# Split output weights for all twelve channel blocks in the last batch, eight factor sets, and a planner that knows more of what a product waits for

## The chip, the cores and the metric

One core of a Trainium2 chip runs the whole kernel. The metric is the device time of one execution in microseconds (us). The profile below is of one execution; the other times are of runs without it. Lower is better.

## The reference

An attention block with 32 inducing points feeds a SwiGLU block. There are 4 batches of 12416 rows with 128 channels, so 49664 rows go through the second block.

```python
def mab(q, kv):
    s = scale * (q @ kv.transpose(0, 2, 1))
    s = s - s.max(-1, keepdims=True)
    a = np.exp(s)
    a /= a.sum(-1, keepdims=True) + 1e-09
    return a @ kv
h = mab(I, x)            # I: 32 inducing points, x: the rows of a batch
x = mab(x, h)
...
xn = x / rms * rms_g
g = xn @ w_gate          # 128 -> 1536
silu = g * (1.0 / (1.0 + np.exp(-g)))
val = xn @ w_val         # 128 -> 1536
return (silu * val @ w_out).astype(np.float32)   # 1536 -> 128
```

## The kernel before, in words

**Work and its tiles.** A batch is cut into 7 stages of rows and these into 25 units: 24 of 512 columns (480 in the sixth stage) and one of 256. A unit passes through the second block in 12 channel blocks of 128, so a batch has 300 *slots*, one for each unit and block. In a slot (`slot`, L678) TensorE makes the gate product (L681) and the value product (L692), ScalarE the silu (L689), and VectorE multiplies the two (L698). The result, u, is one operand of the output product with the block's part of `wo`, which is summed over the 12 blocks in the PSUM tile `acc`. When a unit's twelve are in, `finish` (L622) adds and turns it, and four DMAs store it.

**Plain and split blocks.** A plain block does the output product in fp32 (`project`, L617; TensorE runs it as two instructions, so the profile counts it twice). A split block replaces it by three products of fp32r operands: `three` (L655) makes three factors (hi, lo, d) of u, and `project3` (L633) multiplies them with three parts of the weights; two go to the PSUM tile `u3`, the third to `acc`. ScalarE copies u3 when a unit's last split product is in (L642). Two kinds: by *sums*, u stays in PSUM, ScalarE makes hi (L663), VectorE lo (L664), GpSimd d (L673); by *differences*, ScalarE makes d and hi (L667, L672) and GpSimd lo and d (L668, L673). The factors lie in a ring of four sets (`RING`), in the room of x's row tiles xn2 to xn4. The weights' parts are made in slots 17 to 24 of the first batch (`split_wo`, L570) for the first ten of twelve channel blocks (`NK = NJ - 2`); blocks 10 and 11 are always plain.

**The head.** The weights come as 64-bit floats, and each of nine chunks of 512 columns is rounded to fp32 in steps (`rounding`, L214: power, power_number, upper, upper_number, sign, lower), the last of which is a multiplication on GpSimd (L283). The gate and value chunks are then multiplied with the first batch's h (`stack_of`, L469) to make the stationary operands sg and sv, and are copied to DRAM on SP's queue (`put`, L219) for the later batches. The first chunk of each lies in a borrowed tile. For the others `power` allocates "home", a tile of four chunks in the room of xn1. `stack_of` removes chunks from `w0`, and "home" is allocated again whenever the chunk (0, 1) is not in it.

**What sets the order.** Each engine executes its instructions in the order in which the program issues them, and the order is written out. `schedule` (L825) gives each step of the attention of the next batch a slot; `seam` (L487) is the rest of the attention that belongs to a stage, down to a moving operand for the gate and value products. `rehearse` (L931) goes through all slots with costs and keeps a clock for each engine. It decides which blocks are split and in which way (`decide`, L1040, with `fits`, L1026, which asks how far VectorE, ScalarE and GpSimd would fall behind), and at which place TensorE gets each output product: ahead of a slot's gate product or of its value product (`picks`). Before the value product it takes products only as long as a reserve of 7 stays over (`RESERVE`, with exceptions). Products are then issued in this order (`products`, L1144), and a product that is not ready stops all later work on TensorE.

Of the kernel before, what the change touches and what calls it, by code (L numbers as in the profile page):

```python
# [18 lines left out]
P = 128  # L19
# [4 lines left out]
def kernel(  # L24
# [189 lines left out]
    def rounding(i, c):  # L214
# [20 lines left out]
        def power():  # L235
            if i < 2:
                if not c:
                    t = silp.tile([P, 512], F32, name="silu") if i else halves.tile([P, 512], F32, name="lo")
                    w0[i, c] = t[:]
                else:  # L240
                    if (0, 1) not in w0:
                        w0["home"] = xnp.tile([P, 4, 512], F32, name="xn1")
                    w0[i, c] = w0["home"][:, 2 * (c - 1) + i, :]
                dst = st["dst"] = w0[i, c]
            else:
                dst = st["dst"] = wo.rearrange("p j c -> p (j c)")[:, ts(c, 512)]
            if not wide:
                nc.sync.dma_start(out=dst if i < 2 else dst.rearrange("p (j c) -> p j c", c=C), in_=source(i, c))
                return
            words = raw[i, c].rearrange("p (f w) -> p f w", w=2)  # L250
            st["low"], st["high"] = words[:, :, 0], words[:, :, 1]
            e = st["e"] = work.tile([P, 512], I32, name="we", tag="work")
            nc.vector.tensor_scalar(out=e[:], in0=st["high"], scalar1=20, scalar2=0x7FF,
                                    op0=ALU.logical_shift_right, op1=ALU.bitwise_and)
# [315 lines left out]
    def split_wo(step):  # L570

        if not step:
            kws["first"] = xnp.tile([P, half + NK, C], F32R, name=f"xn{full - 1}")
            for name in ("hi", "lo", "d"):
                kws[name] = xnp.tile([P, RING, 512], F32R, name=f"xn{full - 4 + len(kws) - 2}")

        def part(kind, g):
            n = kind * NK + g * half
            t = kws["first"][:, n:n + half, :] if n < half + NK else kws["more"][:, n - half - NK:n - NK, :]
            return t, t.bitcast(F32)  # L580

        def scaled(kind, g, mul, src=None):
            to, now = part(kind, g)
            nc.scalar.activation(to, now if src is None else src, AF.Copy, scale=mul)

        for g in range(2):
            one = wo[:, g * half:(g + 1) * half, :]
            at = step - g
            if at == 0:
                scaled(0, g, 1.0 - 2.0 ** -13, one)  # L590
            if at == 1:
                nc.gpsimd.tensor_tensor(out=part(1, g)[0], in0=one, in1=part(0, g)[1], op=ALU.subtract)
            if at == 3:
                scaled(1, g, 4096.0)
            if at == 4:
                nc.gpsimd.tensor_tensor(out=part(2, g)[0], in0=part(1, g)[1], in1=part(0, g)[1], op=ALU.subtract)
            if at == 6:
                scaled(0, g, 4096.0)

    def weight_of(kind, j):  # L600
        n = kind * NK + j
        return kws["first"][:, n, :] if n < half + NK else kws["more"][:, n - half - NK, :]

    def ffn(b, u):
# [28 lines left out]
        def project3(j, hi, lo, d):  # L633
            if st["k"] == nk:
                st["u"] = ps_u.tile([P, 512], F32, name="u3")
            ups = st["u"]
            nc.tensor.matmul(ups[:, 0:T], weight_of(0, j), hi, start=st["k"] == nk, stop=False)  # L637
            st["k"] -= 1
            nc.tensor.matmul(ups[:, 0:T], weight_of(1, j), lo, start=False, stop=not st["k"])  # L639
            if not st["k"]:  # L640
                o = st["o"] = outp.tile([P, 512], F32, name="o")
                nc.scalar.activation(o[:, 0:T], ups[:, 0:T], AF.Copy, scale=1.0 + 2.0 ** -12)  # L642
            project(weight_of(2, j), d)
            kws["out"] -= 1
# [10 lines left out]
        def three(j, t):  # L655

            assert kws.get("out", 0) < RING
            kws["out"] = kws.get("out", 0) + 1
            n = kws["n"] = (kws.get("n", 0) + 1) % RING
            hi, lo, d = (kws[name][:, n, 0:T] for name in ("hi", "lo", "d"))  # L660
# [9 lines left out]
            def rest():  # L670
# [3 lines left out]
                kara.append(lambda: project3(j, hi, lo, d))  # L674
# [128 lines left out]
    if B > 1:  # L803
        for _ in range(R):
# [8 lines left out]
            "lower": (0, .6, 0, 1.26), "stack_of": (.87, 0, .5), "stack_low": (0, .62), "split_wo": (0, 0, .7, 1.52)}  # L813
    BANKS = {"scores1", "sum_h", "max2", "max3", "fold_l", "turn_h", "square_h", "stack", "scores2", "square", "stack_of"}
    ENGINES = ("PE", "DVE", "ACT", "POOL")
# [9 lines left out]
    def schedule(b):  # L825
# [19 lines left out]
        if not b:  # L845
# [14 lines left out]
            marks.append(exponentials(3 * NS + 9, f["exp2"], 1))  # L860
        if b + 1 < B:
# [69 lines left out]
    def rehearse():  # L931
# [3 lines left out]
        taken = [0.0] * SILU  # L935
        queues, uses, later, left = {"plain": [], "three": []}, [0], [], {}
        split = {"out": 0, "u3": 0.0, "all": 0, "made": 0}
# [11 lines left out]
        def has(kind, by):  # L949
            return bool(queues[kind]) and queues[kind][0][0] <= by  # L950
# [4 lines left out]
        def issue(kind, to):  # L955
# [6 lines left out]
            else:  # L962
                if st["three"] == 0:
                    run("PE", 0, split["u3"])
# [4 lines left out]
                st["open"] -= 1  # L969
            st["left"] -= 1  # L970
# [3 lines left out]

        def close(unit, w):
            st = left[unit]
            if st["three"]:
                split["u3"] = run("ACT", 0.47 * w, st["end"])

            def finish():  # L980
                run("DVE", 0.6 * w, st["end"], split["u3"])
                soon(1, lambda: run("DVE", 0.63 * w))

            soon(1, finish)
# [22 lines left out]
        def do(name):  # L1007
            cost = COST.get(name, ())
            t = 0.0
            if name == "turn_z" or name == "stack_low":  # L1010
# [4 lines left out]
                return  # L1015
            i = bank() if name in BANKS else None
            for e, us in zip(ENGINES, cost):
                if us:
                    t = run(e, us, t, free[i]) if e == "PE" and i is not None else run(e, us, t)
# [20 lines left out]
        def decide(b, k, u, j):  # L1040
            n = b * NU * NJ + k
            if (j >= NK or b == 0 and (u < 2 or k < 26) or (b, u) == flat[-1] and j > 6 or split["out"] > RING or
# [6 lines left out]
        def slot(b, k, u, j, tanh):  # L1049
            w = per2[units[u][0]] * m / 512.0  # L1050
            st = left.setdefault((b, u), dict(left=NJ, three=0, open=0, all=False, slots=0, end=0.0))
            kind = decide(b, k, u, j)
            first, second = picks[b, k] = [], []
# [7 lines left out]
            least = 1 if near(b, k, 0, 4) or (b, u) == flat[-1] else RESERVE + 2 * near(b, k, -2, 0)  # L1061
# [5 lines left out]
            while split["made"] == RING and any(one[0] == 1 and one[1].__name__ == "three" for one in later):  # L1067
# [13 lines left out]
            names = [step.__name__ for step, _ in given(b, k, u, j)]  # L1081
            for name in names:
                if name in ("exp1_of", "exp2") and k in plans[b][1]:
                    run("ACT", 1.28)
                do(name)
# [27 lines left out]
            if st["slots"] == NJ:  # L1113
                st["all"] = True
                if not st["left"]:
# [9 lines left out]
    for b in range(B):  # L1125
# [3 lines left out]
        for k, (u, j) in slots(b):  # L1129

            def steps():
# [7 lines left out]
                for step, args in given(b, k, u, j):  # L1139
# [4 lines left out]
            def products(some):  # L1144
                for kind in picks[b, k][some]:
# [39 lines left out]
```

## Time and profile before

| what | value |
|---|---|
| timed runs | 1637.60, 1638.86, 1640.44 us (median 1638.86) |
| profiled execution | 1637.58 us, span of the instructions 1635.7 us |
| TensorE clock granted | 1.00 |
| silu x gate slots | 1200, of them 706 split |
| DMA traffic | 112.52 MB, 49 GB/s of HBM over the span |

Engines in the profile: PE is TensorE's matmuls and PEld its weight loads, which overlap them; DVE is VectorE, ACT ScalarE, POOL GpSimd, SP the queue that issues most DMAs. A group of instructions reads line, engine, operation, written tile <- read tiles, shapes, count | busy time, mean ns of one | idle time ahead of it and what ended it. Matmuls are pipelined, and their recorded durations overlap; the time from one start to the next shows what one costs. In the program's names, `xn` is any tile in the room of x's rows: the factors and the split weights lie there too, as does the rounded weights' "home".

### The profile page before, as it was taken

What the parts mean: (1) busy time and instruction counts of PE and PEld (TensorE: products, weight loads), DVE (VectorE), ACT (ScalarE), POOL (GpSimd) and SP (SyncE); (2) the same over time, 40 slices, a digit from 0 to 9 for tenths busy, and PEclk for the clock granted to TensorE, in tenths of its full rate; (3) what the DMA queues carried; (4) which work ended last, traced back from release to release, by engine and by line L of the source; (5) the groups of instructions that cost most, each with busy time, mean ns of one, the idle gap of its engine ahead of it and who ended that gap; (6) DMA issues with size and microseconds to landing.
All of it is one profiled execution on the core that took longest, in us unless ns stands there. A gap on an engine that the chain in (4) does not pass through costs nothing.

```text
span 1635.7 us, 25441 instructions
## 1 busy us (share of the span) xinstructions
PE 1608.4 (98%) x7086; PEld 1084.5 (66%) x7086; DVE 1444.4 (88%) x2506; ACT 1246.0 (76%) x2285; POOL 1217.5 (74%) x979
## 2 busy tenths in 40 slices
PE   8899999999999999999999999999999999999998
PEld 6546666766676666765667666676567776677776
DVE  4878988899899997889899998789989999999997
ACT  4567888767787778777778787777778788778786
POOL 1348895878588886688767897577858878878876
PEclk9999999999999999999999999999999999999999
DMA  6455534433454241624335324253221122112211
GB/s 260 90 72 81 90 62 85 102 90 63 65 88 69 40 88 26 135 58 103 63 67 84 57 39 87 49 131 77 51 38 29 29 40 38 34 35 38 39 36 27
DMA packets 389181, 112.52 MB, mean 69 GB/s; under 512 B 365072, under 2 KB 369712, under 8 KB 386480
## 3 DMA queue, kind: packets, MB, share of 16 engines
q1 hardware_dynamic: 388304, 110.82, 34.6%
q8 instruction: 56, 0.92, 0.2%
q14 instruction: 85, 0.70, 0.2%
q10 hardware_dynamic: 736, 0.08, 0.0%
HBM read 53.95 MB, written 27.00 MB: 49 GB/s over the span
## 4 chain that ended last, share of the span: by engine, by line
PE 85%; DVE 4%; issue 3%; ACT 2%; POOL 2%; DMA 1%; SPq 0%; DVEq 0%; ACTq 0%; POOLq 0%
PE acc L617 31%; PE gv L681 16%; PE gv L692 15%; PE u L637 9%; PE u L639 9%; PE gv L326 3%; PE gv L503 1%; DVE gv L698 1%; PE gv L382 1%; ACT silu L689 1%; DVE u L698 1%; POOL rs L520 1%; POOL xn L673 1%; DVE xn L664 1%; PE gv L457 0%
## 5 line engine op out<-in xcount | busy, mean ns | idle before, releaser
L673 POOL TENSOR_TENSOR xn<-xn,xn 128x512 fp32r<-128x512 f32 (+2 forms) x706 | 872.0, 1255 | 305.9 <-DVE xn L664 169.5
L689 ACT ACTIVATE silu<-gv 128x512 f32<-128x512 f32 (+2 forms) x1186 | 691.5, 586 | 271.9 <-PE gv L681 242.5
L692 PE MATMUL gv<-a,sv 128*128 128x512 f32 (+2 forms) x1188 | 634.9, 534 | 2.4 <-ACT silu L689 2.2
L681 PE MATMUL gv<-a,sg 128*128 128x512 f32 (+2 forms) x1188 | 489.6, 412 | 1.9 <-ACT silu L689 0.8
L617 PE MATMUL acc<-u,wo 128*128 128x512 f32 (+2 forms) x988 | 489.5, 580 | 0.0
L698 DVE TENSOR_TENSOR u<-silu,gv 128x512 f32<-128x512 f32 (+1 forms) x619 | 407.3, 664 | 53.9 <-PE gv L692 33.3
L698 DVE TENSOR_TENSOR gv<-silu,gv 128x512 f32<-128x512 f32 (+2 forms) x567 | 378.5, 669 | 77.0 <-PE gv L692 55.7
L664 DVE SCALAR_TENSOR_TENSOR xn<-xn,gv 128x512 fp32r<-128x512 f32 (+2 forms) x568 | 373.1, 657 | 9.0 <-ACT xn L663 6.2
L663 ACT ACTIVATE xn<-gv 128x512 fp32r<-128x512 f32 (+2 forms) x568 | 332.2, 585 | 41.3 <-DVE gv L698 31.2
L681 PEld LDWEIGHTS gv<-a,sg 128*128 128x128 f32 x1188 | 223.7, 188 | 187.2 <-ACT silu L689 40.4
L692 PEld LDWEIGHTS gv<-a,sv 128*128 128x128 f32 x1188 | 223.7, 188 | 142.6 <-issue 48.9
L617 PE MATMUL acc<-xn,more 128*128 128x512 f32 (+2 forms) x706 | 275.1, 390 | 6.1 <-POOL xn L673 2.9
L637 PE MATMUL u<-xn,xn 128*128 128x512 f32 (+2 forms) x706 | 272.9, 387 | 0.9 <-ACT o L642 0.7
L617 PEld LDWEIGHTS acc<-u,wo 128*128 128x128 f32 x988 | 184.6, 188 | 46.3 <-issue 9.4
L668 POOL TENSOR_TENSOR xn<-u,xn 128x512 fp32r<-128x512 f32 (+1 forms) x138 | 177.3, 1285 | 5.4 <-ACT xn L667 5.4
L639 PE MATMUL u<-xn,xn 128*128 128x512 f32 (+2 forms) x413 | 159.8, 387 | 0.1
L617 PEld LDWEIGHTS acc<-xn,more 128*128 128x128 f32 x706 | 132.5, 188 | 40.8 <-POOL xn L673 13.4
L637 PEld LDWEIGHTS u<-xn,xn 128*128 128x128 f32 x706 | 132.7, 188 | 31.2 <-issue 4.6
L639 PE MATMUL u<-xn,more 128*128 128x512 f32 (+2 forms) x293 | 113.3, 387 | 0.0
L667 ACT ACTIVATE xn<-u 128x512 fp32r<-128x512 f32 (+1 forms) x138 | 87.0, 630 | 30.0 <-DVE u L698 23.1
L520 POOL TENSOR_TENSOR rs<-ms,mhalf 128x16 f32<-128x16 f32 (+2 forms) x28 | 75.9, 2710 | 25.2 <-DVE ms L515 24.8
L639 PEld LDWEIGHTS u<-xn,xn 128*128 128x128 f32 x413 | 77.5, 188 | 17.5 <-POOL xn L668 0.5
(151 smaller groups left out, 1092.2 us busy)
## 6 DMA issues: line engine op xcount, KB each, us to landing
out_dram<-o SPq DMA_DIRECT2D x320, 64.0 KB, 2.0
xT<-in_x_dram SPq DMA_DIRECT2D x60, 256.0 KB, 5.1
xn<-in_x_dram SPq DMA_DIRECT2D x60, 256.0 KB, 4.9
a<-hi SPq DMA_DIRECT2D x156, 64.0 KB, 2.0
a<-lo SPq DMA_DIRECT2D x156, 64.0 KB, 2.0
xn<-in_x_dram SPq DMA_DIRECT2D x5, 1024.0 KB, 10.2
xn<-w SPq DMA_DIRECT2D x18, 256.0 KB, 3.5
out_dram<-o SPq DMA_DIRECT2D x64, 60.0 KB, 2.0
```

The costliest lines, as they stand in the source:

```text
L520: nc.gpsimd.tensor_tensor(out=rs, in0=st["ms"], in1=mhalf[rows, 0:n], op=ALU.pow)
L617: nc.tensor.matmul(acc[:, 0:T], lhsT, rhs, start=st["left"] == NJ, stop=st["left"] == 1)
L637: nc.tensor.matmul(ups[:, 0:T], weight_of(0, j), hi, start=st["k"] == nk, stop=False)
L639: nc.tensor.matmul(ups[:, 0:T], weight_of(1, j), lo, start=False, stop=not st["k"])
L663: nc.scalar.activation(hi, v, AF.Copy, scale=(1.0 - 2.0 ** -13) * 2.0 ** -12)
L664: nc.vector.scalar_tensor_tensor(out=lo, in0=hi.bitcast(F32), scalar=-4096.0, in1=v, op0=ALU.mult, op1=ALU.add)
L668: nc.gpsimd.tensor_tensor(out=lo, in0=v, in1=d.bitcast(F32), op=ALU.subtract)
L673: nc.gpsimd.tensor_tensor(out=d, in0=hi.bitcast(F32), in1=lo.bitcast(F32), op=ALU.subtract)
L681: nc.tensor.matmul(g[:, 0:T], sg[:, ts(j, P)], a[:, 0:T], start=True, stop=True)
L689: nc.scalar.activation(sl[:, 0:T], g[:, 0:T], AF.Silu)
L692: nc.tensor.matmul(v[:, 0:T], sv[:, ts(j, P)], a[:, 0:T], start=True, stop=True)
L698: nc.vector.tensor_tensor(out=t[:, 0:T], in0=sl[:, 0:T], in1=v[:, 0:T], op=ALU.mult)
```

## The change

It has these parts:

- In the last batch x's turned sets (tiles xT0 to xT6) are no longer needed for a next batch. `split_last`, in slots 2, 4 and 6 of that batch, makes split weights for blocks 10 and 11 in xT0's room, and four more factor sets in the rooms xT1 to xT3. From slot 10 of that batch on `decide` may split all twelve blocks, and up to eight sets may be out.
- Factor sets are taken from a list and put back when the three products are issued, instead of by a running number.
- The four gate and value chunks that lay in "home" get a tile each, in the rooms xn1 to xn4.
- The rehearsal knows more of what a step waits for (`AFTER`, `done`), and fills TensorE's waits ahead of attention's products with output products; these are issued between the steps (`products(n + 2)`). It makes the copy of u3 when a unit's last split product is in and not when the unit closes, and does not offer a unit's first split product before u3 is free.
- The reserve is 3 instead of 7 in the first 16 slots of the first batch.

```diff
         def power():
             if i < 2:
-                if not c:
-                    t = silp.tile([P, 512], F32, name="silu") if i else halves.tile([P, 512], F32, name="lo")
-                    w0[i, c] = t[:]
-                else:
-                    if (0, 1) not in w0:
-                        w0["home"] = xnp.tile([P, 4, 512], F32, name="xn1")
-                    w0[i, c] = w0["home"][:, 2 * (c - 1) + i, :]
+                t = (xnp.tile([P, 512], F32, name=f"xn{2 * c - 1 + i}") if c else
+                     silp.tile([P, 512], F32, name="silu") if i else halves.tile([P, 512], F32, name="lo"))
+                w0[i, c] = t[:]
...
-            for name in ("hi", "lo", "d"):
-                kws[name] = xnp.tile([P, RING, 512], F32R, name=f"xn{full - 4 + len(kws) - 2}")
+            rings = [xnp.tile([P, RING, 512], F32R, name=f"xn{full - 4 + n}") for n in range(3)]
+            kws["sets"] = [[ring[:, n, :] for ring in rings] for n in range(RING)]
...
+    def split_last(step):
+
+        n = NJ - NK
+        if not step:
+            kws["last"] = xtp.tile([P, 3 * n, C], F32R, name="xT0")
+            rings = [xtp.tile([P, RING, 512], F32R, name=f"xT{n + 1}") for n in range(3)]
+            kws["sets"] += [[ring[:, n, :] for ring in rings] for n in range(RING)]
+        one, (whi, wlo, ws) = wo[:, NK:NJ, :], (kws["last"][:, ts(kind, n), :] for kind in range(3))
+        if step == 0:
+            nc.scalar.activation(whi, one, AF.Copy, scale=1.0 - 2.0 ** -13)
+            nc.gpsimd.tensor_tensor(out=wlo, in0=one, in1=whi.bitcast(F32), op=ALU.subtract)
+        if step == 1:
+            nc.scalar.activation(wlo, wlo.bitcast(F32), AF.Copy, scale=4096.0)
+            nc.gpsimd.tensor_tensor(out=ws, in0=wlo.bitcast(F32), in1=whi.bitcast(F32), op=ALU.subtract)
+        if step == 2:
+            nc.scalar.activation(whi, whi.bitcast(F32), AF.Copy, scale=4096.0)
+
     def weight_of(kind, j):
+        if j >= NK:
+            return kws["last"][:, kind * (NJ - NK) + j - NK, :]
...
-            assert kws.get("out", 0) < RING
-            kws["out"] = kws.get("out", 0) + 1
-            n = kws["n"] = (kws.get("n", 0) + 1) % RING
-            hi, lo, d = (kws[name][:, n, 0:T] for name in ("hi", "lo", "d"))
+            where = kws["sets"].pop(0)
+            hi, lo, d = (one[:, 0:T] for one in where)
...
+    AFTER = {"max2": "max1", "max3": "max2", "fold_l": "exp1_of", "turn_h": "divide", "square_h": "turn_h", "square": "turn_a",
+             "sum_h": "turn_e", "scores1": "turn_x", "stack": "turn_h", "root": "scale", "apply": "root"}
...
+        if b + 1 == B:
+            for step in range(3):
+                add(2 + 2 * step, split_last, step)
...
+            t, unit = queues[kind][0][:2]
+            if kind == "three" and not left[unit]["three"]:
+                t = max(t, split["u3"])
+            return t <= by
...
+        def copy(st, w):
+            if st["all"] and st["three"] and not st["open"] and "u3" not in st:
+                st["u3"] = split["u3"] = run("ACT", 0.47 * w, st["end"])
...
+            t = done.get(args if name == "stack_of" else AFTER.get(name), 0.0)
             i = bank() if name in BANKS else None
             for e, us in zip(ENGINES, cost):
+                if us and e == "PE":
+                    t = max(t, free[i])
+                    fill(to, t)
                 if us:
-                    t = run(e, us, t, free[i]) if e == "PE" and i is not None else run(e, us, t)
+                    t = run(e, us, t)
...
-            if (j >= NK or b == 0 and (u < 2 or k < 26) or (b, u) == flat[-1] and j > 6 or split["out"] > RING or
+            if (j >= (NJ if b + 1 == B and k > 9 else NK) or b == 0 and (u < 2 or k < 26) or (b, u) == flat[-1] and j > 6 or split["out"] > split["room"] or
...
+            if b + 1 == B and k == 3:
+                split["room"] = 2 * RING
...
-            least = 1 if near(b, k, 0, 4) or (b, u) == flat[-1] else RESERVE + 2 * near(b, k, -2, 0)
+            least = (1 if near(b, k, 0, 4) or (b, u) == flat[-1] else 3 if not b and k < 2 * NJ - 8 else
+                     RESERVE + 2 * near(b, k, -2, 0))
...
-                for step, args in given(b, k, u, j):
+                for n, (step, args) in enumerate(given(b, k, u, j)):
+                    products(n + 2)
                     step(*args)
```

## The prediction

> **What bounds the kernel now.** I read the page's first and fourth parts, then the timeline of TensorE in a quiet stretch, then TensorE's waits, then the stages where it waits.
>
> ```profile
> PE 1608.4 (98%) x7086; PEld 1084.5 (66%) x7086; DVE 1444.4 (88%) x2506; ACT 1246.0 (76%) x2285; POOL 1217.5 (74%) x979
> PE 85%; DVE 4%; issue 3%; ACT 2%; POOL 2%; DMA 1%; SPq 0%; DVEq 0%; ACTq 0%; POOLq 0%
> ```
>
> TensorE is busy nearly all the time and holds 85% of the chain that ended last; the next engine, VectorE, has 12% to spare. A busy TensorE can still hide slack, so I price its work by starts, in a stretch of the timeline where nothing waits:
>
> ```profile
> 902.02 1.02 PE L617 MATMUL acc<-u,wo 128*128 128x512 f32 x2
> 902.48 0.80 PE L692 MATMUL gv<-a,sv 128*128 128x512 f32 x1
> 903.11 0.40 PE L681 MATMUL gv<-a,sg 128*128 128x512 f32 x1
> 903.35 0.40 PE L637 MATMUL u<-xn,xn 128*128 128x512 f32 x1
> 903.58 0.39 PE L639 MATMUL u<-xn,xn 128*128 128x512 f32 x1
> 903.81 0.40 PE L617 MATMUL acc<-xn,more 128*128 128x512 f32 x1
> 904.05 0.39 PE L692 MATMUL gv<-a,sv 128*128 128x512 f32 x1
> ```
>
> Columns: start, duration, engine, line, operation. The three factor matmuls of a split block (L637, L639, L617) start 0.23 us apart. A plain block is one fp32 product in two records; from its start to the gate product at 903.11 are 1.09 us, of which 0.23 belong to the value product between. So a plain block costs 0.86 us and a split block 0.70: **0.16 us for each block that is split**. With 480 columns the chain has 0.81 against 3 x 0.22, 0.15 us.
>
> TensorE's own waits, then the largest of them in TensorE's and GpSimd's timelines:
>
> ```profile
> PE gv L471 <- POOL xn L283: 3.7, 1, 3.7
> PE acc L617 <- POOL xn L673: 2.9, 8, 0.9
> PE acc L617 <- DVE o L625: 2.7, 3, 0.9
> PE gv L692 <- ACT silu L689: 2.2, 8, 0.5
> ```
>
> ```profile
> 69.28 0.40 PE L692 MATMUL gv<-a,sv 128*128 128x512 f32 x1
> 73.39 1.13 PE L471 MATMUL gv<-xn,hg 128*128 128x512 f32 x2 [3.71 <-POOL xn L283]
> ```
>
> ```profile
> 71.79 1.55 POOL L283 TENSOR_TENSOR xn<-o,we 128x512 f32<-128x512 f32 x1 [6.66 <-DVE u L698]
> 75.53 1.29 POOL L283 TENSOR_TENSOR xn<-o,we 128x512 f32<-128x512 f32 x1 [2.19 <-DMA w<-xn]
> ```
>
> The whole kernel has one long TensorE wait, in the head: a weight chunk is not there for stack_of. GpSimd's part of that chunk could have run when VectorE's lower step (68.63, 0.69 us) ended, about 69.35, but started at 71.79. In the listing of instructions it waits for two DMAs: "home" was allocated again in the same room, so the write waits until the earlier chunks' copies to DRAM have been read out, and SP's queue was held by four loads of x (issued 59.47, for 7.3 us). Last, the stages (TensorE, weight loads, VectorE, ScalarE, GpSimd; first the head, then the last batch):
>
> ```profile
> 55.00:70.00 15.00, 13.41 (x39) 6.55 (x38) 13.25 (x23) 9.03 (x18) 3.72 (x4) 1.00 0.89 158
> 1261.00:1635.70 374.70, 366.18 (x1430) 263.49 (x1428) 340.97 (x573) 295.00 (x551) 298.48 (x238) 1.00 0.19 35
> ```
>
> **What the Trainium skill says.** "FP8 and Floating Point Precision", TensorE Precision Notes, gives true fp32 four passes through the array; the trace agrees roughly, 0.86 against 0.23 us, 3.7 times. "Perfetto Trace Analysis", Identifying the Most-Contended Engine, warns that TensorE's busy share is no measure of its headroom; hence the starts. "GPSIMD Engine Reference", Elementwise, puts a two-input tensor_tensor at about 2.6 cycles an element, which would be an estimated 1.1 us for 512 at its 1.2 GHz; the trace has 1.25 from start to start (four in 5.04 us), and I use that.
>
> **The change, part by part.** The planner decides which blocks are split and where each product stands, so I counted instructions of both listings.
>
> *Splits.* In the last batch 35 blocks of numbers 10 and 11 are newly split, but 14 fewer of the other ten, because the planner still asks whether VectorE, ScalarE and GpSimd keep up: 219 split blocks instead of 198. The other batches have -1, +1 and +1: 728 instead of 706. TensorE: 18 x 0.16 + 3 x 0.15 in the last batch and 0.16 in the others, 3.5 us. The very end is not bound by TensorE (after 1620 it waits for silu and VectorE), so I take **-3.0** (bounds -3.5 and 0).
>
> *What they cost elsewhere.* The 21 are 7 by sums and 14 by differences. GpSimd: 21 x 1.25 + 14 x 1.37 (the timeline's 1340.96 to 1342.33), 45 us, and two subtractions of 256 columns for the new weights (0.74 each, as L673 at 256): 298 + 47 = 345 of some 370 us, 93%. VectorE: 7 x 0.60 (start to start), 4 us. ScalarE: 7 x 0.49 + 14 x 1.05, 18 us, and three scalings of 256 columns at 0.38: 314, 85%. All three stay below TensorE's 363, so their work lies beside it; what can surface is lateness, priced below. split_last stands in slots 2, 4 and 6 of the batch; xT0 to xT3 were last read by scores2 in the batch before, so it waits for nothing, and behind its GpSimd part stand only factor products.
>
> *Eight sets.* A set is written again after twice as many blocks, so fewer factor steps wait for TensorE (L673 waits for gate products 13.8 us in this batch, off the path). Priced 0, hidden beside TensorE's stream.
>
> *The head.* Four chunks get rooms of their own (xn1 to xn4), whose first users, the x rows, are done; GpSimd's write then comes at about 69.35 and ends at 70.7. Besides, four products are moved: to slots 3, 6, 8 and 11 from slots 16 to 19 (the lower reserve), 4 x 0.86 = 3.4 us of TensorE work ahead of the late stack_of. TensorE's work up to it grows from about 11.6 to 15.0 us, from 55.1 to about 70.9 with some small waits left, so the 3.7 us and some of the 1.7 us of smaller waits ahead of it (0.99 at 60.98 is the largest) go. Against this, slots 16 to 19 now hold only gate and value products, 4 x 0.46 + 0.53 for the scores = 2.4 us of TensorE beside 4 x 0.60 + 1.2 = 3.6 us of VectorE, and VectorE was 88% busy up to 70. So some 1.2 us and a little lateness come back: 3.7 + 1.0 - 1.4 = **-3.3** (bounds 0, if VectorE is the bound there, and -5.5). The DMAs of the chunks keep their place on SP; the rings take the rooms xn2 to xn4 only from slot 26 on.
>
> *Order of products.* The planner now knows when attention's steps and u3 are ready, and exchanges a split product for a plain one in some 300 of 1200 slots. Where the trace has a wait and the place changes: slot 42 of the first batch,
>
> ```profile
> 123.76 0.39 PE L637 MATMUL u<-xn,xn 128*128 128x512 f32 x1
> 124.20 0.50 PE L639 MATMUL u<-xn,xn 128*128 128x512 f32 x1
> ...
> 125.56 0.50 PE L617 MATMUL acc<-xn,more 128*128 128x512 f32 x1 [0.85 <-POOL xn L673]
> ```
>
> two factor products 0.2 and 1.1 us late, now a plain one: **-1.0**. Slots 139 and 170 of the first three batches (0.3 to 0.7 and 0.4 us): 3.2 us, of which I take 60%, **-1.9**. Five of the ten waits of the last batch behind a seam (0.2 to 0.4 each, 1.8 us; GpSimd's root takes 2.9): half, **-0.9**. The three of 1.05 us at slot 5 of the later batches stay: nothing is moved there. What the exchanges put elsewhere the trace cannot show; I take **+1.5** for new waits of this kind (bounds 0 and +4). *The end.* The last product is now a split one behind the plain ones, and ScalarE's copy of u3 (0.38) follows it: **+0.5**.
>
> Sum: -3.0 - 3.3 - 1.0 - 1.9 - 0.9 + 1.5 + 0.5 = **-8.1 us** on the span of 1635.7, to 1627.6. The median of the timed runs is 3.2 us above that span, so the forecast is 1638.9 - 8.1 = **1630.8**.
>
> **Rivals.** (B) *Only the work counts.* VectorE is the bound in the head, the wait at 73.39 comes back in slots 16 to 19, and new waits cancel the removed ones: 1638.9 - 3.5 = 1635.4. For it VectorE's 88%; against it that 3.7 us are idle on TensorE, and VectorE is only 63% busy from 81 to 90 (5.66 of 9). (C) *All listed waits go, none come:* 3.5 + 5.5 + 1.3 + 3.2 + 1.8 - 2 for the end and the slots without products = 13: 1626. (D) *Slower: GpSimd becomes the last batch's bound.* It has 345 us of work, and had 76 us of idle time before, most of it waiting for VectorE's L664, which is fed by ScalarE and TensorE in turn. If more than about 25 us of that cannot be filled, GpSimd passes TensorE, and each product it delivers late stops TensorE in order; with half (38 us) the batch takes 383 instead of 375: 1639 + 8 - 3 in the head = 1644. Against it: eight sets let GpSimd run behind without stopping anyone, and the planner's split limit counts its load. (E) *It doesn't do what it says:* the listing rules that out in kind, not in size: a net 21 and not 35.
>
> **How the numbers follow.** A 0.62 (own range 1628 to 1633.5), B with E 0.20, C 0.13, D 0.05. The range 1625 to 1635.5 takes in C and most of B; left out are D and a part of B. About 0.2% (3.3 us) is what a measurement of this kernel can tell from no change, so faster means below 1635.6: A, C and half of B, 0.85; same 0.10; slower 0.05.
>
> **What would show it.** L617's plain records fall from 988 to 944; stack_of's wait for GpSimd (3.7) is gone and no TensorE wait above 1 us appears in slots 16 to 19; GpSimd is some 93% busy in the last batch and TensorE there waits for L673's successor no more than the 3 us it does now; the last batch is 3 to 4 us shorter, the head 3, the middle batches about 1 each. A longer last batch with GpSimd back to back would prove D; an unchanged end of the head's scores (84.6) would prove B.

## The result, and the profile after

The changed kernel takes **1623.22 us** (median of 5 runs, 1623.03 to 1623.65) against 1638.86 before: a ratio of 0.9905, 95% interval 0.989 to 0.9919. The forecast of 1630.8 had the direction, but the time lies 1.8 us below its range. The profiled execution took 1623.65 us with a span of 1621.6, so the span fell by 14.1 us where the sum of the prediction said 8.1. Times of the same kernel go with TensorE's granted clock: executions of the kernel before in the sessions below have a median of 1636.90 us at 1.000 and of 1640.21 us at 0.997 (three each), most lie at 0.999, and the five of the changed kernel are all at 1.000.

The same two lines of the page as before, engines and chain:

```profile
PE 1603.1 (99%) x7108; PEld 1088.4 (67%) x7108; DVE 1451.1 (89%) x2518; ACT 1248.4 (77%) x2320; POOL 1258.5 (78%) x1013
PE 93%; DVE 2%; ACT 1%; issue 1%; POOL 0%; DVEq 0%; ACTq 0%
```

TensorE's share of the chain rose from 85% to 93%: what went is waiting, hardly work. Its list of waits (who waited <- for whom: us in total, times, longest) has lost its two longest lines, those for GpSimd (3.7 and 2.9 us); 0.2 us of such waits is left, at the head's next chunk:

```profile
PE acc L632 <- DVE o L640: 3.5, 5, 0.9
PE gv L322 <- ACT xT L316: 1.5, 2, 0.8
...
PE gv L706 <- ACT silu L703: 1.1, 4, 0.5
PE gv L695 <- ACT silu L703: 1.1, 3, 0.5
```

(L632 is L617 of before, L640 is L625, L687 is L673, L706 and L695 are L692 and L681, L467 is L471.) The head, in GpSimd's timeline and then in TensorE's:

```profile
69.36 1.34 POOL L279 TENSOR_TENSOR xn<-o,we 128x512 f32<-128x512 f32 x1 [4.31 <-DVE o L277]
```

```profile
70.45 0.80 PE L706 MATMUL gv<-a,sv 128*128 128x512 f32 x1
71.09 1.02 PE L467 MATMUL gv<-xn,hg 128*128 128x512 f32 x2
71.54 0.80 PE L695 MATMUL gv<-a,sg 128*128 128x512 f32 x1
```

GpSimd's part of the chunk starts at 69.36, as worked out, ended by VectorE's step and no longer by DMAs; stack_of (L467) follows its neighbour after 0.64 us, with no wait. The two stages (start:end, length, then busy us of TensorE, weight loads, VectorE, ScalarE, GpSimd; last the clock, the DMA share, GB/s):

```profile
55.00:70.00 15.00, 14.54 (x45) 8.06 (x44) 13.36 (x23) 9.07 (x17) 4.22 (x5) 1.00 0.82 155
1249.00:1621.60 372.60, 364.47 (x1451) 266.79 (x1450) 344.42 (x580) 305.05 (x589) 343.67 (x275) 1.00 0.19 35
```

In the same 15 us of the head TensorE does 45 instructions instead of 39. GpSimd's 343.67 us are 92% of the last batch (345 and 93% were forecast), and the list of waits has no matmul of that batch that waits for GpSimd.

**Where the time went.** Every slot begins with a gate product, so the start of the same gate product in both traces shows what has been gained up to there. Worked out from the two traces' rows:

| up to | start before | start after | gained in all |
|---|---|---|---|
| slot 12 of the first batch | 74.0 | 71.5 | 2.4 |
| slot 24 | 94.7 | 89.6 | 5.1 |
| slot 42 | 123.5 | 118.4 | 5.2 |
| slot 48 | 133.0 | 125.9 | 7.1 |
| second batch | 469.5 | 460.8 | 8.8 |
| third batch | 865.4 | 855.0 | 10.4 |
| last batch | 1261.0 | 1249.0 | 11.9 |
| its slot 299 | 1628.3 | 1613.7 | 14.6 |
| end of the span | 1635.7 | 1621.6 | 14.1 |

A second reckoning sets each TensorE instruction at its distance from start to start where nothing waits (as in the prediction, 0.23 us for 512 columns) and calls the rest gaps; the last batch is counted up to the end of TensorE's last product. First batch: gaps 25.1 before, 16.3 after; second and third: 13.9 and 13.7, then 12.5 and 12.4; last: **work 361.9 to 358.5, gaps 7.9 to 9.0**. So the splits saved 3.4 us of work in the last batch and some of it was lost to new gaps there; all else came from gaps.

The two largest new gaps are not GpSimd's. TensorE and VectorE at slot 151 of the last batch:

```profile
1432.75 1.02 PE L632 MATMUL acc<-u,wo 128*128 128x512 f32 x2
...
1434.08 0.39 PE L653 MATMUL u<-xn,xn 128*128 128x512 f32 x1
...
1434.29 0.68 DVE L640 TENSOR_TENSOR o<-acc,o 128x512 f32<-128x512 f32 x1
1434.31 0.40 PE L655 MATMUL u<-xn,xn 128*128 128x512 f32 x1
...
1435.12 0.47 PE L632 MATMUL acc<-xn,more 128*128 128x512 f32 x1 [0.42 <-DVE o L640]
```

`acc` has two PSUM tiles, which the units take in turn. The plain product at 1432.75 is the last of unit 10, issued after all those of unit 11, because the planner takes a ready split product ahead of a plain one. One slot later unit 12 begins (1434.08), and its product into `acc` needs unit 10's tile. VectorE's add L640 reads that tile until 1434.97, so the product comes 0.6 us late by starts (1435.12 - 1434.31 - 0.23). Slot 199 shows the same with 0.7. Two smaller gaps, 0.4 and 0.5 us by starts, lie ahead of the gate products of slots 170 and 221, which wait for ScalarE's silu (0.23 and 0.31 listed).

### The profile page after: what moved, and what is told of

It is laid out like the page before. It is cut to its first block, busy times and chain, and to the rows that moved or that the text cites. A ratio compares the mean times of both kernels' runs of the same rounds, so it can differ in the third digit from the quotient of the medians.

```text
span 1621.6 us, 25590 instructions
## 1 busy us (share of the span) xinstructions
PE 1603.1 (99%) x7108; PEld 1088.4 (67%) x7108; DVE 1451.1 (89%) x2518; ACT 1248.4 (77%) x2320; POOL 1258.5 (78%) x1013
## 4 chain that ended last, share of the span: by engine, by line
PE 93%; DVE 2%; ACT 1%; issue 1%; POOL 0%; DVEq 0%; ACTq 0%
PE acc L632 34%; PE gv L695 18%; PE gv L706 16%; PE u L655 10%; PE u L653 10%; PE gv L322 3%; PE gv L499 1%; PE gv L378 1%; DVE gv L712 1%; ACT silu L703 1%; PE gv L453 0%; DVE o L640 0%; DVE xn L678 0%; PE gv L467 0%; DVE u L712 0%
## 5 line engine op out<-in xcount | busy, mean ns | idle before, releaser
L687 POOL TENSOR_TENSOR xn<-xn,xn 128x512 fp32r<-128x512 f32 (+2 forms) x620 | 766.0, 1254 | 218.9 <-DVE xn L678 125.4
L706 PE MATMUL gv<-a,sv 128*128 128x512 f32 (+2 forms) x1188 | 627.2, 528 | 1.2 <-ACT silu L703 1.1
L695 PE MATMUL gv<-a,sg 128*128 128x512 f32 (+2 forms) x1188 | 489.0, 412 | 1.5 <-ACT silu L703 0.5
L632 PE MATMUL acc<-u,wo 128*128 128x512 f32 (+2 forms) x944 | 467.7, 580 | 0.0
L712 DVE TENSOR_TENSOR u<-silu,gv 128x512 f32<-128x512 f32 (+2 forms) x607 | 397.7, 662 | 57.2 <-PE gv L706 32.2
L712 DVE TENSOR_TENSOR gv<-silu,gv 128x512 f32<-128x512 f32 (+2 forms) x579 | 385.3, 668 | 52.4 <-PE gv L706 38.8
L695 PEld LDWEIGHTS gv<-a,sg 128*128 128x128 f32 x1188 | 223.7, 188 | 189.7 <-ACT silu L703 46.5
L678 DVE SCALAR_TENSOR_TENSOR xn<-xn,gv 128x512 fp32r<-128x512 f32 (+2 forms) x490 | 320.7, 654 | 8.4 <-ACT xn L677 5.1
L677 ACT ACTIVATE xn<-gv 128x512 fp32r<-128x512 f32 (+2 forms) x490 | 285.5, 583 | 38.9 <-DVE gv L712 27.6
L706 PEld LDWEIGHTS gv<-a,sv 128*128 128x128 f32 x1188 | 223.6, 188 | 136.7 <-issue 42.9
L632 PE MATMUL acc<-xn,more 128*128 128x512 f32 (+2 forms) x603 | 233.6, 387 | 3.5 <-DVE o L640 3.5
L653 PE MATMUL u<-xn,xn 128*128 128x512 f32 (+2 forms) x603 | 232.6, 386 | 0.0
L632 PEld LDWEIGHTS acc<-u,wo 128*128 128x128 f32 x944 | 176.4, 188 | 44.7 <-issue 8.9
L682 POOL TENSOR_TENSOR xn<-u,xn 128x512 fp32r<-128x512 f32 (+2 forms) x130 | 167.3, 1287 | 42.2 <-ACT xn L681 42.2
L687 POOL TENSOR_TENSOR xT<-xT,xT 128x512 fp32r<-128x512 f32 (+2 forms) x108 | 135.1, 1276 | 6.9 <-DVE xT L678 4.4
L655 PE MATMUL u<-xn,xn 128*128 128x512 f32 (+2 forms) x351 | 135.6, 386 | 0.0
L632 PEld LDWEIGHTS acc<-xn,more 128*128 128x128 f32 x603 | 113.3, 188 | 29.0 <-POOL xn L687 3.7
L653 PEld LDWEIGHTS u<-xn,xn 128*128 128x128 f32 x603 | 113.4, 188 | 23.3 <-issue 4.4
L681 ACT ACTIVATE xn<-u 128x512 fp32r<-128x512 f32 (+2 forms) x130 | 81.7, 628 | 38.5 <-DVE u L712 35.5
```

The lines of the kernel that those rows point to most:

```text
L632: nc.tensor.matmul(acc[:, 0:T], lhsT, rhs, start=st["left"] == NJ, stop=st["left"] == 1)
L677: nc.scalar.activation(hi, v, AF.Copy, scale=(1.0 - 2.0 ** -13) * 2.0 ** -12)
L678: nc.vector.scalar_tensor_tensor(out=lo, in0=hi.bitcast(F32), scalar=-4096.0, in1=v, op0=ALU.mult, op1=ALU.add)
L681: nc.scalar.activation(d, v, AF.Copy, scale=1.0 - 2.0 ** -13)
L682: nc.gpsimd.tensor_tensor(out=lo, in0=v, in1=d.bitcast(F32), op=ALU.subtract)
L687: nc.gpsimd.tensor_tensor(out=d, in0=hi.bitcast(F32), in1=lo.bitcast(F32), op=ALU.subtract)
```

## The experiments

All ratios are to the kernel before, whose median in these sessions was 1638.69 to 1638.75. Up to slot 0 TensorE does the same in all these kernels, and yet that slot's gate product starts between 54.3 and 55.5 us; differences of that size between spans are not the edits'. Where a stretch is compared, it is therefore counted from slot 0's gate product. "Gaps" and "work" are of TensorE in the last batch, reckoned as above.

### The rooms of the chunks

**Rooms alone.** The kernel before, in its order of products, with a tile of its own for each of the four chunks.

```diff
-                if not c:
-                    t = silp.tile([P, 512], F32, name="silu") if i else halves.tile([P, 512], F32, name="lo")
-                    w0[i, c] = t[:]
-                else:
-                    if (0, 1) not in w0:
-                        w0["home"] = xnp.tile([P, 4, 512], F32, name="xn1")
-                    w0[i, c] = w0["home"][:, 2 * (c - 1) + i, :]
+                t = (xnp.tile([P, 512], F32, name=f"xn{2 * c - 1 + i}") if c else
+                     silp.tile([P, 512], F32, name="silu") if i else halves.tile([P, 512], F32, name="lo"))
+                w0[i, c] = t[:]
```

> The kernel before with only the four chunks' own rooms; TensorE's order of instructions is the one of before. Theory (late chunk): GpSimd's write for chunk (0, 2) comes when VectorE's lower ends, about 69.35 instead of 71.79, TensorE's wait for stack_of falls from 3.7 to about 1.2 us, and the span by about 2.5, to 1633.2. Rival (VectorE bounds the head): less than 0.7 us is gained, since VectorE's queue sets the later slots.

1635.80 us, 0.9981 (0.9972 to 0.9989); span 1634.3. Its waits:

```profile
PE gv L467 <- POOL xn L279: 1.6, 2, 1.2
```

The wait of 3.7 us fell to 1.2 and 0.4. By the gate products 2.6 us were gained up to slot 12 and 0.7 given back by slot 24, so 1.9 remain. The room takes away GpSimd's wait for the DMAs; but TensorE, with no more to do ahead of stack_of, is there too early.

**The shared room put back** into the changed kernel (the same diff, reversed).

> The changed kernel with the shared home tile of before; TensorE's order is the one of the changed kernel. Theory (late chunk): stack_of of chunk (0, 2), at 71.1 in the changed kernel, waits for GpSimd until about 73.3, some 2.2 us, and the span is 1621.6 + 2 = 1623.6. Rival (the products moved ahead hide it all): no more than 0.5 us is lost.

1627.69 us, 0.9926 (0.9909 to 0.9942); span 1626.1, 4.5 above the changed kernel's. TensorE's wait, and GpSimd's for the copies to DRAM, which this trace names (that of before put it down to VectorE):

```profile
PE gv L471 <- POOL xn L283: 2.0, 1, 2.0
71.65 1.41 POOL L283 TENSOR_TENSOR xn<-o,we 128x512 f32<-128x512 f32 x1 [6.79 <-DMA w<-xn]
```

2.3 us are lost by slot 12 and 1.1 more by slot 24. The other 1.1 us of the 4.5 were not lost in the head but in the last three batches, 0.3 to 0.5 in each, where the order is the same; the profiled execution had a clock of 0.998, the changed kernel's 1.000. The only one of the four at 1.000 took 1625.76 us with a span of 1623.6, which is the 2 us that the theory gave. So room and order help each other: up to slot 24 the room is worth 1.9 us in the old order and 3.4 in the new one (one trace each).

**The reserve of 7 put back** in the first 16 slots.

```diff
-            least = (1 if near(b, k, 0, 4) or (b, u) == flat[-1] else 3 if not b and k < 2 * NJ - 8 else
-                     RESERVE + 2 * near(b, k, -2, 0))
+            least = 1 if near(b, k, 0, 4) or (b, u) == flat[-1] else RESERVE + 2 * near(b, k, -2, 0)
```

> The changed kernel with the old reserve of 7 in the first 16 slots; the rest of the order is the same. The planner then puts two or three products directly ahead of stack_of in slots 11 and 13 instead of one a slot earlier. Theory (only that TensorE has work ahead of the late stack_of counts): no more than 1 us slower, since the fill ahead of stack_of does the same. Rival (the reserve is what carries the head): some 3 us slower, with TensorE waits back in slots 4 to 11.

1624.42 us, 0.9911 (0.9897 to 0.9926); span 1622.6. Only 1.0 us, 0.7 of it by slot 24: without the lower reserve the planner's fill ahead of stack_of moves the products there all the same. The reverse holds too: without the fill and with the lower reserve (next run) the head loses nothing. The kernel with neither, and the rooms, wasn't tried.

### What the planner knows

**Without the times of attention's chains** (no AFTER and no fill in the rehearsal), the rest as changed.

```diff
-            t = done.get(args if name == "stack_of" else AFTER.get(name), 0.0)
+            t = 0.0
...
-                if us and e == "PE":
-                    t = max(t, free[i])
-                    fill(to, t)
                 if us:
-                    t = run(e, us, t)
+                    t = run(e, us, t, free[i]) if e == "PE" and i is not None else run(e, us, t)
```

> The changed kernel, but the rehearsal does not know what attention's steps wait for and puts no product ahead of them. Theory (this part removes the waits for GpSimd behind root at slots 42 and 170): these come back, 1.3 + 3 x 0.4 us, and some in the last batch, span about 1624.5. Rival (the new handling of u3 does it all): no more than 0.5 us slower.

1630.14 us, 0.9948 (0.9931 to 0.9964); span 1628.2, 6.6 above the changed kernel's. TensorE's timeline at slot 42 of the first batch, first of this kernel:

```profile
118.17 0.40 PE L695 MATMUL gv<-a,sg 128*128 128x512 f32 x1
118.40 0.39 PE L653 MATMUL u<-xn,xn 128*128 128x512 f32 x1
118.86 0.49 PE L655 MATMUL u<-xn,xn 128*128 128x512 f32 x1
120.21 0.50 PE L632 MATMUL acc<-xn,more 128*128 128x512 f32 x1 [0.86 <-POOL xn L687]
```

then of the changed one, with a plain product in that place:

```profile
118.37 0.40 PE L695 MATMUL gv<-a,sg 128*128 128x512 f32 x1
118.61 1.02 PE L632 MATMUL acc<-u,wo 128*128 128x512 f32 x2
119.06 0.80 PE L706 MATMUL gv<-a,sv 128*128 128x512 f32 x1
```

The wait for GpSimd's factor behind a seam is back: 1.7 us by slot 48. At slot 170 of each of the first three batches 0.6 us return, and the last batch is 3.5 us longer up to slot 299, 2.5 of it before slot 60, most at slots 27 and 34 (gaps 12.0). The loss is more than twice what was expected. The times of the chains and the fill were taken out together, so what each is worth stays open.

**With the old idea of u3** as well as without the last batch's part. Shown against the version without the part (below).

```diff
-            t, unit = queues[kind][0][:2]
-            if kind == "three" and not left[unit]["three"]:
-                t = max(t, split["u3"])
-            return t <= by
+            return queues[kind][0][0] <= by
...
+                if st["three"] == 0:
+                    run("PE", 0, split["u3"])
                 end = run("PE", 0.697 * w, t)
...
-                st["end"] = end
-                copy(st, w)
...
+            if st["three"]:
+                split["u3"] = run("ACT", 0.47 * w, st["end"])
...
-                copy(st, w)
```

> The changed kernel without the last batch's part, and with the planner's old idea of when u3 and its copy are ready; its knowledge of attention's chains stays. 709 split blocks; only 58 slots differ from the kernel before. Against the version without the last batch's part (span 1621.8). Theory: the waits at slots 64, 89 and 139 of the first three batches (0.2, 0.5 and 0.7 us before the change), which stayed away when the attention chains' times were taken out of the planner, come back: 3 x 1.2 = 3.6 us, less 4 splits (0.6), so span 1624 to 1626, with nothing lost at slot 42 and in the head. Rival: those waits went by the mere exchange of places, and the knowledge of attention explains all of it: span 1621 to 1622.

1627.66 us, 0.9933 (0.9919 to 0.9947); span 1625.8, 4.0 above the version that it is compared with, as the first theory said. In the second batch gaps at slots 64, 89 and 139 are back with 0.34, 0.58 and 0.77 us, the sizes of before (0.34, 0.59, 0.77). Over the first three batches it loses 3.8 us. Slot 42 and the head lose nothing.

### The last batch

**Without its part**: no split_last, ten blocks, four sets.

```diff
-        if b + 1 == B:
-            for step in range(3):
-                add(2 + 2 * step, split_last, step)
...
-            if (j >= (NJ if b + 1 == B and k > 9 else NK) or b == 0 and (u < 2 or k < 26) or (b, u) == flat[-1] and j > 6 or split["out"] > split["room"] or
+            if (j >= NK or b == 0 and (u < 2 or k < 26) or (b, u) == flat[-1] and j > 6 or split["out"] > split["room"] or
...
-            if b + 1 == B and k == 3:
-                split["room"] = 2 * RING
```

> The changed kernel without split_last: ten blocks and four sets in the last batch too, 705 split blocks instead of 728. Theory (the splits pay 0.155 us each, and the waits for GpSimd that the last batch of the changed kernel shows, 2.3 us, are their price): 3.5 - 2.3 and some for waits that go otherwise, 1 to 2 us slower, span 1623.1. Rival (work alone counts): 3.5 us slower, 1625.1. Rival (the last batch gains by the planner alone): no slower.

1623.24 us, 0.9902 (0.9887 to 0.9917); span 1621.8. **The same time as with it.** By the reckoning work is 3.7 us more (362.2 for 358.5; 23 splits fewer, so 0.16 each), gaps 3.7 less (5.3 for 9.0).

**Twelve blocks, four sets** (the changed kernel without the four more).

```diff
-            kws["sets"] += [[ring[:, n, :] for ring in rings] for n in range(RING)]
...
-            if b + 1 == B and k == 3:
-                split["room"] = 2 * RING
```

> The changed kernel with twelve blocks but four sets in the last batch: 712 split blocks; in the order no unit's first product stands within three slots of the close of the unit that used its accumulator before, save the one at slot 5. Theory (the last batch's new waits are waits for one of two accumulators, because eight sets let split products pass an older unit's plain ones): against the kernel without the last batch's part 7 more splits (-1.1) and three waits of 0.24 us less (-0.7), span about 1620, 1.6 us faster than the changed kernel. Rival (the waits come of VectorE's and GpSimd's load): about as the changed kernel, 1621.5.

1623.13 us, 0.9905 (0.989 to 0.992); span 1621.8. The theory missed here, and the time is the rival's: against the version without the part, work is 1.1 us less (361.1) and gaps 0.9 more (6.2). The three waits that were to go are gone, and the list names no new one for an accumulator. What makes the new gaps, each below 0.5 us, wasn't found.

**Ten blocks, eight sets.**

```diff
-            if (j >= (NJ if b + 1 == B and k > 9 else NK) or b == 0 and (u < 2 or k < 26) or (b, u) == flat[-1] and j > 6 or split["out"] > split["room"] or
+            if (j >= NK or b == 0 and (u < 2 or k < 26) or (b, u) == flat[-1] and j > 6 or split["out"] > split["room"] or
```

> The changed kernel with its eight sets, but blocks 10 and 11 stay plain: 714 split blocks, 209 of them in the last batch (the version without all of the last batch's part has 705 and 200, the changed one 728 and 223). Theory (accumulators): the planner's order now lets a unit's first product follow one slot after the last product of the unit two before, which has the same accumulator, at slots 53, 101, 149, 197 and 245 of the last batch; each should show a TensorE wait of 0.5 to 0.7 us for VectorE's add, about 3 us, so the 9 additional splits (1.4 us) are paid back: span 1622 to 1623.5, against 1621.8 without the part. Rival (only the work and GpSimd's lateness count): 9 splits give 1.4 us and GpSimd, less loaded than in the changed kernel, stops nobody: span 1620.4 or less, no waits at those five slots.

1629.35 us, 0.9942 (0.993 to 0.9955); span 1626.7. The waits stand at exactly the five slots named, but each is 1.6 us and not 0.5 to 0.7. The list of waits, then slot 101 in the timeline:

```profile
PE acc L632 <- DVE o L640: 9.7, 8, 1.4
```

```profile
1373.66 0.69 DVE L712 TENSOR_TENSOR gv<-silu,gv 128x512 f32<-128x512 f32 x1
...
1373.86 0.40 PE L655 MATMUL u<-xn,xn 128*128 128x512 f32 x1
...
1374.27 0.68 DVE L678 SCALAR_TENSOR_TENSOR xT<-xT,gv 128x512 fp32r<-128x512 f32 x1
1374.87 0.68 DVE L640 TENSOR_TENSOR o<-acc,o 128x512 f32<-128x512 f32 x1
...
1375.70 0.47 PE L632 MATMUL acc<-xn,more 128*128 128x512 f32 x1 [1.44 <-DVE o L640]
```

The add that frees the tile is issued behind the slot's multiplication and a factor (L712, L678), so it is the third of VectorE's queue and ends at 1375.55. The wait is that queue, not the add alone; it was priced as the add alone. GpSimd, with 316.64 us of work in 378.5, 84%, is less loaded than in the changed kernel, and the batch is longer.

**The older unit's product first**, in the last batch of the changed kernel.

```diff
+        def oldest(now):
+            kinds = [kind for kind in ("three", "plain") if has(kind, now)]
+            return min(kinds, key=lambda kind: max(queues[kind][0][1], (B - 1, 0)), default=None)
...
-                if has("three", now):
-                    issue("three", to)
-                elif has("plain", now):
-                    issue("plain", to)
-                else:
+                kind = oldest(now)
+                if kind is None:
                     break
+                issue(kind, to)
...
-                kind = next((kind for kind in ("three", "plain") if has(kind, now)), None)
+                kind = oldest(now)
```

> The changed kernel, and in the last batch the planner prefers, of two ready products, the one of the older unit: 729 split blocks, and no unit's first product closer than 12 slots to the close of the accumulator's last user, save slot 5. Theory (accumulators): the waits at slots 151 and 199 (0.53 and 0.69) go, and what of the others hangs on them; 1.2 to 2.5 us faster than the changed kernel, span 1619 to 1620.4. Rival (load of VectorE and GpSimd): no faster, 1621.6.

**1620.33 us**, 0.9887 (0.9873 to 0.9902); span 1618.3. This is faster than both kernels. Its last batch:

```profile
1248.80:1618.30 369.50, 362.97 (x1452) 266.87 (x1450) 344.92 (x584) 305.80 (x587) 340.70 (x273) 1.00 0.19 36
```

Work is the same (358.4), gaps fall from 9.0 to 5.8, and slots 151 and 199 wait no more. These two were 1.3 us; the rest of the 3.3 us of span, more than was expected, came with other places: the waits for silu at slots 170 and 221 are gone too, and 1.6 us were gained after slot 280. GpSimd does nearly the same work (340.70 us for 343.67) in a batch 3 us shorter, so its load wasn't what held the changed kernel.

**The same order without the part**: the version with ten blocks and four sets, and the older unit first (the same diff).

> The changed kernel without the last batch's part (ten blocks, four sets), but with the older unit's ready product issued first in the last batch. 677 split blocks, 172 in the last batch: with the older unit first, four sets fill up and 28 fewer blocks are split than without that order (200). With all of the last batch's part the same order kept 224 and measured a span of 1618.3. Theory (the part needs the order and the order needs the part): 28 x 0.16 = 4.5 us more work, and the waits of about 1 us at slots 53, 149 and 245 go, so span 1625 to 1627, some 8 us above the version that has both. Rival (the order is what gained, the part is worth nothing in any order): span about 3 us below the version without the part, 1618 to 1620.

1633.30 us, 0.9967 (0.9955 to 0.998); span 1631.3, 9.5 above the version without the order. The 28 splits fewer are 4.5 us of work (366.7 for 362.2), as expected. The other 5 us were not: gaps rise from 5.3 to 10.8, about 0.3 us each at the value products of 17 slots, mostly twelve apart. Slot 47:

```profile
1306.72 0.60 ACT L677 ACTIVATE xn<-gv 128x512 fp32r<-128x512 f32 x1 [1.31 <-DVE gv L712]
1307.22 1.09 ACT L703 ACTIVATE silu<-gv 128x512 f32<-128x512 f32 x2
1307.86 0.19 PEld L706 LDWEIGHTS gv<-a,sv 128*128 128x128 f32 x1 [0.58 <-ACT silu L703]
```

The value product's weight load waits for ScalarE's silu; ScalarE had stood for 1.31 us at a factor (L677) that waited for VectorE's multiplication (L712), which follows the finished unit's add (L640, 1305.32 to 1306.00) in VectorE's queue. Slot 59 shows the same chain. That the add's place causes it wasn't tested. So the order alone loses 9.5 us of span and the part alone gains nothing, but together they gain about 3 (1620.33 us against 1623.24).

**Twelve blocks on the kernel before**, with its planner and four sets.

```diff
+        if b + 1 == B:
+            for step in range(3):
+                add(2 + 2 * step, split_last, step)
...
-            if (j >= NK or b == 0 and (u < 2 or k < 26) or (b, u) == flat[-1] and j > 6 or split["out"] > RING or
+            if (j >= (NJ if b + 1 == B and k > 9 else NK) or b == 0 and (u < 2 or k < 26) or (b, u) == flat[-1] and j > 6 or split["out"] > split["room"] or
```

> The kernel before with split weights for twelve blocks in the last batch, with its four sets and its planner: 713 split blocks instead of 706. Theory (work): 7 x 0.155 = 1.1 us faster than before, span 1634.6. Rival (order decides): the new order of the last batch changes the span by more than 1 us in either direction beside that.

1642.77 us, 1.0021 (1.0013 to 1.003): **slower**; span 1639.4. Seven more splits save 1.2 us of work (360.7), and the gaps grow from 7.9 to 13.0, with one of 1.9 us at slot 65 where a unit's first product follows one slot after its tile's last. With the old planner the part loses; what the planner learned is what makes it free.

## Why the prediction missed

The direction and most places of the gains were right. What failed is the sizing of the waits that go: the exchanges (-1.9, measured -4.8), the head (-3.3, measured -5.0) and slot 42 (-1.0, measured -2.0), together 5.6 of the 6.0 us by which the sum on the span was short. In the last batch the cause of the new waits was wrong besides. Term by term:

| term | forecast | measured (gate products) |
|---|---|---|
| head, to slot 24 | -3.3 | -5.0 |
| slot 42 | -1.0 | -2.0 |
| rest of the first three batches | -1.9 | -4.8 |
| last batch to slot 299: splits, seams, new waits | -3.0 - 0.9 + 1.5 = -2.4 | -2.7 |
| end | +0.5 | +0.5 |

- **Head: two terms mis-sized, "+ 1.0" and "- 1.4".** Up to slot 12 TensorE needs 2.3 us less and does 3.4 us more (the four products), so 5.7 us of waits went: the 3.7 and 2.1 of the smaller ones, of which I had taken 1.0. Against this I let 1.4 us come back in slots 16 to 19, because they have no output products and VectorE was 88% busy. From slot 16's to slot 20's gate product the two traces have 6.51 and 3.31 us: 3.2 less, where 3.44 us of products were moved out. So 0.25 came back there, and 0.5 at slot 13. VectorE is as busy as before from 55 to 70 us (13.36 us for 13.25), and it did not bound the slots behind. The room carries 3.4 us of the head (shared room put back) and the reserve 0.7.
- **Slot 42.** Both late factor products were read, but the gap at slot 48 (0.6 us, gone after the change) was not, and the list shows less than a wait costs: 0.85 us in brackets is 1.13 by starts (1.36 us from 124.20 to 125.56, less 0.23). Of the 2.0 us, 1.7 return without the knowledge of attention's chains.
- **Exchanges: mis-sized, the largest part of the miss.** I counted the waits at slots 139 and 170 and took 60% of them. The runs show that the planner's knowledge of u3 removed 3.8 us in these batches, slots 64 and 89 among them, and its knowledge of attention 0.6 at each slot 170, 1.8 in all: 5.6 for the two, of which the whole change keeps 4.8. Neither the many waits under 0.6 us nor their full removal was priced; there was no reason in the profile for 60%.
- **New waits +1.5.** In the first three batches few showed. One is at slot 43 of the first, where the value product is 0.4 us late by starts and its weight load waits for ScalarE's silu (120.78, 0.66 listed); the list of matmul waits hasn't it at all. In the last batch they came, and the place and cause were wrong: with the part, gaps are 3.7 us above those without it, and the cause shown at slots 151 and 199 (1.3 us of them) is the accumulator and not a late factor. That kind stood in the list of before, as the three waits of L617 for L625 at slot 5, which I counted only as staying. The new gaps ate what the splits saved (3.7 us), while the rest of the change had removed 2.6 us of gaps (7.9 before, 5.3 without the part). The forecast for the last batch came near by luck: these errors cancel.
- **Splits.** 21 more in the last batch, as counted, and the starts in the trace after give the same prices (1.09 us for a plain and a value product from 70.00, 0.23 between factor products). The reckoning of work rests on these prices; it doesn't test them. The plain records fell to 944, as forecast.
- **From span to median.** I carried 3.2 us from before; it was 1.6 after, since the profiled execution of before lay 1.3 us below its own median, at a clock of 1.00, and that of after 0.4 above its own. That is the other 1.6 us of the 7.6. The clocks given at the top fit it; whether the change has a part in them isn't shown.

Rival C (1626, all listed waits go and none come) was nearest in number, 1622.7 against 1621.6 on the span, but not in kind: new waits did come, and the list shows those that went too small. B fell: the head's scores, whose place was its sign, start at 80.36 instead of 84.60. D had the load right (92%) and its consequence wrong: TensorE's waits for GpSimd are gone from the last batch, and the faster order does nearly the same GpSimd work in less time. The estimate of 1.1 us from "GPSIMD Engine Reference", Elementwise, lies below the trace after as well, whose 620 records of L687 have a mean of 1.25 us. The load was forecast with the trace's 1.25, 345 us in all, and 343.67 was measured.

What stays open: why the version with four sets, 0.6 us ahead of the changed kernel by slot 240 of the last batch, loses 1.2 us to it by slot 299; what else the faster order removed, besides the waits named above; and whether a third accumulator would do as well as the order, which wasn't tried.

## What to carry to other kernels

When more work becomes movable, look at what closes the work already open: with two accumulators, a planner that prefers the fast kind of product leaves the last slow one of the older unit lying, and the next unit waits for the tile. An edit that saves work and one that orders it can each be worth nothing or less and gain only together (here 0 and -9.5 us, and about 3 gained with both), so test the pairs. And read waits by starts, including the small repeated ones: a list of the longest shows neither their number nor their full cost.

## What the runs showed of the hardware

A matmul's record ends later than the next one could start (0.40 us recorded, 0.23 from start to start), so a wait in the profile is 0.17 us or more shorter than its cost: 0.42 against 0.6 at slot 151, 1.44 against 1.6 at slot 101. "Perfetto Trace Analysis", Identifying the Most-Contended Engine, warns of TensorE's busy share; this case adds that its listed waits are short as well. A write to a tile that DMAs still read waited for them: GpSimd's wait of 6.79 us ended with them when the chunks shared a room, and with VectorE's step, at 69.36, when they had rooms of their own. And kernels that do the same up to slot 0 reach it 54.3 to 55.5 us into the span, so a difference of up to 1.2 us between single spans need not be the edit's.
